# First unit of an attention-plus-experts kernel as eight block products, and the second batch's first two chunks moved to the end of the pair

## Chip, cores and metric

The kernel runs on one core of a Trainium2 chip. The metric is device time in microseconds. Before the change the median of three runs is 1271.27 us (1271.16 to 1274.32).

## What is computed

There are two stages, over 8 batches, 8 heads, 576 tokens and head size 64. Attention runs twice: 32 pack queries p attend to k and v, and the 576 tokens q then attend to the 32 packed rows. The result, laid out as 4608 tokens x 512, goes through four dense experts, weighted by normalised probabilities:

```python
p_packed = sm_attn(p, k, v)
out = sm_attn(q, p_packed, p_packed)          # x: (4608, 512)
p = domain_probs / (domain_probs.sum(-1, keepdims=True) + 1e-09)
for e in range(4):
    h = np.maximum(x @ w1[e], 0.0)            # (4608, 1024)
    y += p[:, e:e+1] * (h @ w2[e])            # (4608, 512)
```

## The kernel before

**Folding.** The second attention has only 32 rows per head, so its value product is folded into w1: `g_form` (line 370) multiplies the packed rows (`ppbd`) with a chunk of w1 and yields `ghl`. The first expert layer then multiplies `ghl` with the softmax weights of the tokens (`xh`, `xl`). Every fp32 operand of the large products is split into a rounded high part (a cast, `hi_of`) and the rest as a low part (a subtraction, `lo_of`), and a product takes three matmuls: high x low, high x high, low x high.

**Units.** The 4 x 1024 hidden columns are cut into eight chunks of 512 (`NCH`). A *unit* is one chunk of one batch: `units` (lines 403 and 404) lists (pair of batches, chunk, batch). Before the change the list begins with batch 0's chunks 0 and 1, batch 1's chunks 1 and 0, and goes on chunk by chunk, batch 0 and 1 in turn; the three later pairs run through chunks 0 to 7.

**First layer.** `mm1_group(u, kh, c)` (line 422) makes one of four blocks of a unit's hidden matrix, half `c` of the tokens (288 columns) by half `kh` of the chunk: 12 matmuls, then one VectorE instruction (relu and probability, from `pbt`). The blocks are a11, a12 (left token half) and a21, a22 (right).

**Second layer.** A unit's product with w2 has the same 2 x 2 block form and is done with seven products instead of eight, in the order `ORDER` (line 35): a11, s3, s1, s2, a22, s4, a12, where the s are sums and differences of the blocks. `s_operand` (line 472) splits an operand, cast on ScalarE and subtraction on GpSimd; `split` (line 414) does it for a12, with the subtraction on VectorE. `product(u, i)` (line 535) issues 12 matmuls; the first of a batch is copied into an accumulator (`acc`), later ones are added by VectorE. The last unit alone uses eight block products, summed in PSUM (`last_unit`, line 577). `combine` (line 607) makes the four output blocks from the seven accumulators at a batch's end.

**Weights.** `t_form` (line 504) makes the seven prepared forms of a w2 chunk (`tt`): seven casts on ScalarE, seven subtractions and four differences on GpSimd. In the first pair each chunk's forms are made and stored to `td` in DRAM (`t_store`); the later pairs load them (`t_load`). The pool has ten `tt` buffers, the raw w2 halves (`rw0`, `rw1`) one each, raw w1 (`wraw`) four.

**The opening** (lines 664 to 721) runs batch 0's attention, with the tokens in halves (`tok_halves`, line 303), loads batch 1's, makes chunk 0's forms, folds chunk 0 for batch 0 and issues the four first-layer groups of unit 0. The left token half's groups, a11 and a12, can run before the right half's softmax is done.

**Order.** TensorE's order is that of the text: `together` (line 121) closes what came before it, `mm` adds to it. `InOrder` fixes VectorE's and GpSimd's order in the opening while `on` is set; `Behind` keeps attention and preparation behind the sums. The loop at line 743 runs the units: product i, the operand two products ahead, parts of the fold (`gsteps`), the next unit's groups (`GROUPS`), a step of the second batch's or the next pair's attention (`back`), and a step of `t_form` (`FORM`). SP issues nearly all DMAs, in order.

## Time and profile before

| what | value |
| --- | --- |
| median of three runs | 1271.27 us |
| lowest, highest run | 1271.16, 1274.32 us |
| profiled execution, its own time | 1272.35 us |
| span of the profiled execution | 1270.6 us |
| mean granted TensorE clock | 0.997 |
| TensorE, VectorE, GpSimd, ScalarE busy | 98%, 73%, 58%, 39% |
| DMA read, written | 173.35 MB, 38.87 MB |

All durations in the rows belong to the one profiled execution. The page names a group by line, engine, operation and tiles; the line of a matmul is that of the helper that issued it (L116 the plain ones, L119 transposes, L124 those issued together), L68 is the helper that fixes an order, so groups are best told apart by tiles: `dbl` is any PSUM tile, `st` and `stl` split operands, `ablk` and `sblk` blocks and sums, `ghl` the folded w1, `xh` and `xl` the token weights, `pbt` the probabilities, `rw` raw w2, `wraw` raw w1. PE is TensorE, PEld its weight load, DVE VectorE, ACT ScalarE, POOL GpSimd, SPq SP's queue. Matmuls overlap, so the busy time of one is longer than the distance to the next.

### The profile page before, as it was taken

Reading aid. Unit: us, or ns where it says so; the run is one execution under the profiler, and the core shown is the slowest. Engines: PE = TensorE matmul, PEld = TensorE weight load, DVE = VectorE, ACT = ScalarE, POOL = GpSimd, SP = SyncE. Lnnn points to the kernel's source line nnn. Section 1 sums busy time; section 2 is a strip of 40 time slices with the busy share of each in tenths; the row PEclk is TensorE's granted clock in tenths of the full one; section 3 lists DMA queues with packets and bytes.
Section 4 is the critical chain, followed back from the end, with each engine's and each line's share of the span. In section 5 each row is a group of like instructions: output and inputs, shape, how many; then the busy total and the mean of one; then the engine's idle time right before and its main releaser. Section 6 shows DMA issues by size and latency. Waiting matters only on the chain.

```text
span 1270.6 us, 26902 instructions
## 1 busy us (share of the span) xinstructions
PE 1247.0 (98%) x10732; PEld 1166.7 (92%) x10732; DVE 926.1 (73%) x1389; ACT 496.1 (39%) x847; POOL 735.8 (58%) x529
## 2 busy tenths in 40 slices
PE   6899999999999999999999999999999999999998
PEld 3789899999999999999999999999999999999998
DVE  6675676788876667888777676788877567766766
ACT  2554445344435233343335433243343533323331
POOL 3876978798675344455466344364557545445456
PEclk9899999999999999999999999999999999999999
DMA  9665575536466444555345555433445543444322
GB/s 339 242 250 200 218 236 177 193 123 213 161 211 209 163 160 127 181 175 165 125 150 175 175 196 165 159 115 116 159 159 182 159 139 116 123 151 159 126 67 76
DMA packets 86508, 213.98 MB, mean 168 GB/s; under 512 B 8816, under 2 KB 27632, under 8 KB 86384
## 3 DMA queue, kind: packets, MB, share of 16 engines
q1 hardware_dynamic: 85712, 212.11, 50.3%
q8 instruction: 86, 1.41, 0.5%
q14 instruction: 38, 0.31, 0.1%
q10 hardware_dynamic: 672, 0.15, 0.1%
HBM read 173.35 MB, written 38.87 MB: 167 GB/s over the span
## 4 chain that ended last, share of the span: by engine, by line
PE 91%; POOL 2%; DMA 2%; DVE 2%; issue 1%; ACT 0%; SPq 0%; DVEq 0%; POOLq 0%; ACTq 0%
PE dbl L116 85%; PE dbl L124 6%; POOL st L68 1%; DMA rw<-in_w 1%; PE dbl L119 1%; DMA pbt<-pnd 1%; DMA vt<-in_v 1%; DVE a L68 1%; POOL tt L68 1%; POOL acc L68 0%; DVE dbl L68 0%; DVE sblk L68 0%; DVE s L68 0%; POOL rw L68 0%; ACT st L151 0%
## 5 line engine op out<-in xcount | busy, mean ns | idle before, releaser
L116 PE MATMUL dbl<-st,tt 128*128 128x288 f32 x4608 | 665.7, 295 | 3.5 <-DVE acc L68 1.8
L116 PEld LDWEIGHTS dbl<-st,tt 128*128 128x128 f32 x4608 | 623.1, 188 | 38.6 <-POOL st L68 19.2
L68 POOL TENSOR_TENSOR st<-sblk,st 128x576 fp32r<-128x576 f32 x252 | 364.7, 1458 | 435.9 <-ACT st L151 434.6
L116 PE MATMUL dbl<-xh,ghl 128*128 128x288 f32 x2048 | 414.4, 295 | 0.0
L68 DVE TENSOR_TENSOR acc<-dbl,acc 128x576 f32<-128x576 f32 x390 | 292.3, 750 | 93.0 <-PE dbl L116 90.6
L116 PEld LDWEIGHTS dbl<-xh,ghl 128*128 128x128 f32 x2048 | 328.9, 189 | 0.2 <-DVE ghl L68 0.2
L116 PE MATMUL dbl<-xl,ghl 128*128 128x288 f32 x1024 | 303.3, 296 | 6.0 <-POOL xl L68 5.7
L151 ACT CAST st<-sblk 128x576 fp32r<-128x576 f32 x252 | 164.1, 675 | 362.6 <-DVE sblk L68 290.9
L68 POOL TENSOR_TENSOR st<-ablk,st 128x576 fp32r<-128x576 f32 x128 | 187.2, 1463 | 47.8 <-ACT st L151 47.7
L116 PEld LDWEIGHTS dbl<-xl,ghl 128*128 128x128 f32 x1024 | 193.1, 189 | 8.7 <-POOL xl L68 6.4
L68 DVE SCALAR_TENSOR_TENSOR dbl<-dbl,pbt 128x576 f32<-128x576 f32 x128 | 97.8, 764 | 75.7 <-PE dbl L116 74.5
L68 DVE SCALAR_TENSOR_TENSOR ablk<-dbl,pbt 128x576 f32<-128x576 f32 x128 | 96.4, 753 | 65.5 <-PE dbl L116 63.0
L151 ACT CAST st<-ablk 128x576 fp32r<-128x576 f32 x128 | 86.1, 674 | 123.7 <-PE dbl L116 92.4
L116 PE MATMUL dbl<-stl,tt 128*128 128x288 f32 x780 | 114.6, 296 | 0.0
L116 PEld LDWEIGHTS dbl<-stl,tt 128*128 128x128 f32 x780 | 105.9, 188 | 0.2
L68 DVE TENSOR_TENSOR ghl<-dbl,ghl 128x512 fp32r<-128x512 f32 x128 | 84.9, 685 | 25.9 <-ACT ghl L151 25.9
L151 ACT CAST ghl<-dbl 128x512 fp32r<-128x512 f32 x128 | 72.2, 590 | 52.9 <-DVE ghl L68 52.2
L68 POOL TENSOR_TENSOR tt<-rw,tt 128x512 fp32r<-128x512 f32 x57 | 74.2, 1321 | 18.7 <-ACT tt L85 18.7
L68 DVE TENSOR_TENSOR stl<-dbl,stl 128x576 fp32r<-128x576 f32 x64 | 48.4, 756 | 39.5 <-ACT stl L151 39.5
L124 PE MATMUL dbl<-wraw,ppbd 64*32 64x512 f32 x1024 | 67.7, 595 | 0.9 <-DMA wraw<-in_w 0.9
L462 ACT COPY sblk<-dbl 128x576 f32<-128x576 f32 x63 | 40.4, 642 | 64.1 <-DVE sblk L68 64.1
L552 ACT COPY acc<-dbl 128x576 f32<-128x576 f32 x56 | 35.9, 641 | 50.9 <-PE dbl L116 50.8
(64 smaller groups left out, 703.1 us busy)
## 6 DMA issues: line engine op xcount, KB each, us to landing
tt<-td SPq DMA_DIRECT2D x175, 512.0 KB, 4.3
wraw<-in_w SPq DMA_DIRECT2D x132, 256.0 KB, 4.3
td<-tt SPq DMA_DIRECT2D x56, 512.0 KB, 5.0
pbt<-pnd SPq DMA_DIRECT2D x32, 288.0 KB, 3.9
out<-acc SPq DMA_DIRECT2D x31, 288.0 KB, 2.6
rw<-in_w SPq DMA_DIRECT2D x16, 512.0 KB, 5.8
kt<-in_k SPq DMA_DIRECT2D x14, 576.0 KB, 5.2
kt<-in_q SPq DMA_DIRECT2D x14, 576.0 KB, 5.8
```

The costliest lines, as they stand in the source:

```text
L68: res = getattr(self.eng, op)(*args, **kw)
L116: on_pe(nc.tensor.matmul(**kw))
L119: on_pe(nc.tensor.transpose(**kw))
L124: ins = nc.tensor.matmul(**kw).ins
L151: return eng.copy(out=dst, in_=src)
L462: nc.scalar.copy(out=held("s1"), in_=psv)
L552: nc.scalar.copy(out=accs[b, i], in_=psv)
```

## The change

- Ten matmuls of the identity with itself are issued as soon as the identity is made, into a PSUM tile that nothing reads.
- In the opening w1's chunk 0 is loaded ahead of w2's, and batch 0's probabilities ahead of batch 1's keys and values. Batch 1's pack scores leave the opening.
- Chunk 0 of w2 is prepared as four plain blocks (`raw_form`: four casts on ScalarE, four subtractions on GpSimd) instead of seven forms.
- Unit 0 uses eight block products (`first_unit`), each pair summed in PSUM: four on the left token half right after a11 and a12, four on the right half between unit 1's first-layer groups. Their results go straight into the four accumulators that `combine` turns into output blocks. The subtractions for a11 and a12 are on GpSimd.
- Batch 1's chunks 0 and 1 move behind chunk 7 of the pair. Chunk 0's seven forms are made there, from a second load of w2; folds for batch 1 alone stand in units 12 and 13. The second pair begins with chunk 1, which is still in the buffers.
- Probabilities are keyed by batch and expert, and the loop's special cases for the first four units become those for the first two.

The diff, cut to its core:

```diff
+FIRST = 10
...
+    ps = dbl()
+    for _ in range(FIRST):
+        nc.tensor.matmul(out=ps[:, 0, 0:P], lhsT=ident, rhs=ident, start=True, stop=True)
...
-    units = [(0, 0, 0), (0, 1, 0), (0, 1, 1), (0, 0, 1)]
-    units += [(sb, ch, 2 * sb + i) for sb in range(SB) for ch in range(2 if sb == 0 else 0, NCH) for i in range(2)]
+    units = [(0, 0, 0), (0, 1, 0)]
+    units += [(0, ch, i) for ch in range(2, NCH) for i in range(2)]
+    units += [(0, 0, 1), (0, 1, 1)]
+    units += [
+        (sb, ch, 2 * sb + i) for sb in range(1, SB) for ch in ((1, 0, *range(2, NCH)) if sb == 1 else range(NCH))
+        for i in range(2)
+    ]
...
-        lo_of(st[:, 1], psv, st[:, 0], vec)
+        lo_of(st[:, 1], psv, st[:, 0], gq if u == 0 and name in ("a11", "a12") else vec)
...
+    def raw_form(ch):
+        raw = [w2r.pop((ch, kh)) for kh in range(2)]
+        for name in ("b11", "b12", "b21", "b22"):
...
+            hi_of(t[:, 0], src, nc.scalar)
+            lo_of(t[:, 1], src, t[:, 0], gq)
+            tt[ch, name] = t
+            yield
...
+    def first_unit():
+        sb, ch, b = units[0]
+        pss = {}
+        for left, n in (
+            ("a11", 1), ("a12", 1), ("a11", 2), ("a12", 2), ("a22", 1), ("a21", 1), ("a22", 2), ("a21", 2),
+        ):
+            r, kh = int(left[1]) - 1, int(left[2])
+            opens = left in ("a11", "a22")
+            st, t = blocks[0, "op", ORDER.index(left) if left in ORDER else left], tt[ch, f"b{kh}{n}"]
+            if opens:
+                pss[r, n] = dbl()
...
+            if not opens:
+                acc = new_acc(b, ORDER.index(RESULT[r, n - 1]))
+                if (r, n) == (1, 1):
+                    nc.scalar.activation(out=acc, in_=ps[:, :, 0:HS], func=AF.Copy, scale=-1.0)
+                else:
+                    nc.scalar.copy(out=acc, in_=ps[:, :, 0:HS])
+                if (r, n) == (1, 2):
+                    other = accs[b, ORDER.index(RESULT[0, 1])]
+                    vacc.tensor_tensor(out=other, in0=other, in1=ps[:, :, 0:HS], op=ALU.subtract)
+            yield
...
+        raws = w1_load(0)
         for kh in range(2):
             w2_load(0, kh, raw_tile)
-        forms = t_form(0, True)
-        raws = w1_load(0)
+        forms = raw_form(0)
         drain(wavefront(packs[:2], 1))
+        load_probs(0, 0)
         for i in (2, 3, 2, 3):
             next(packs[i])
-        load_probs(0, 0)
...
         drain(fold)
         next(halves)
-        next(forms)
-        mm1_group(0, 0, 0)
-        s_operand(0, 0)
-        next(halves)
-        mm1_group(0, 1, 0)
-        for gen in packs[2:]:
-            next(gen)
-        mm1_group(0, 1, 1)
-        mm1_group(0, 0, 1)
-        s_operand(0, 1)
-        vq.on = gq.on = False
-        drain(forms)
+        splits = [mm1_group(0, kh, 0, False) for kh in range(2)]
+        for ready in splits:
+            ready()
+        drain(halves)
...
+    direct = first_unit()
+    for _ in range(4):
+        next(direct)
+    mm1_group(0, 1, 1)
+    mm1_group(0, 0, 1)
+    tsteps = t_form(1)
+    next(tsteps)
+    drain(g_form([0], 1, raws))
+    raws = w1_load(2)
...
+    for i in range(4):
+        next(direct, None)
+        for grp in GROUPS_FIRST[i]:
+            mm1_group(1, *grp)
+        if i:
+            s_operand(1, i - 1)
+        for _ in range((0, 2, 2, 3)[i]):
+            next(back)
+        next(tsteps)
...
+        if u == 1:
+            gsteps, gat = g_form([0, 1], 2, raws), (2,)
+        elif u == 13:
             gsteps, gat = g_form([1], 1, raws), (0,)
+        elif not odd and u + 2 < len(units):
+            gsteps = g_form([1] if u == 12 else [units[u + 2][2], units[u + 3][2]], units[u + 2][1], raws)
+        fch = 2 if u == 1 else (ch + 1) % NCH if sb == 0 and u < 14 else None
...
-            if u < 2 or sb == 0 and u > 3 and not odd:
+            if sb == 0 and (u == 1 or not odd):
                 t_store(ch, i)
-            if u == 2:
-                t_load(0, i)
-            elif odd and not opening and fch is None:
+            if nxt[1] != ch and (nxt[1], i) not in tt:
                 t_load(nxt[1], i)
```

## Rows read from the trace of the kernel before

**Rows 1.** The page, part 1: an engine's busy time in us, its share of the span, its instructions.

```profile
PE 1247.0 (98%) x10732; PEld 1166.7 (92%) x10732; DVE 926.1 (73%) x1389; ACT 496.1 (39%) x847; POOL 735.8 (58%) x529
```

**Rows 2.** The page, part 4: the chain that ended last, shares of the span by engine.

```profile
PE 91%; POOL 2%; DMA 2%; DVE 2%; issue 1%; ACT 0%; SPq 0%; DVEq 0%; POOLq 0%; ACTq 0%
```

**Rows 3.** Busy time of each engine in stretches of the span (us, and the number of instructions in brackets), then the granted clock of TensorE as a share of 2.4 GHz, the share of the 16 DMA engines and GB/s. Stretches overlap a transfer's edge, so the DMA share can exceed 1.

```profile
28.55:33.40 4.85, 0.00 (x0) 0.00 (x0) 4.61 (x10) 1.10 (x2) 4.77 (x5) 1.00 1.06 376
33.40:34.19 0.79, 0.00 (x0) 0.00 (x1) 0.76 (x3) 0.16 (x1) 0.74 (x1) 0.50 1.03 384
34.19:40.20 6.01, 5.89 (x21) 5.23 (x22) 4.15 (x11) 3.60 (x8) 4.84 (x5) 0.50 0.92 362
40.20:67.10 26.90, 25.46 (x275) 21.66 (x275) 16.42 (x30) 15.64 (x30) 23.43 (x19) 1.00 0.65 219
67.10:75.00 7.90, 6.11 (x49) 4.46 (x48) 7.90 (x14) 5.72 (x10) 7.90 (x6) 1.00 1.03 409
...
131.00:138.10 7.10, 5.61 (x59) 3.83 (x58) 3.34 (x6) 4.52 (x9) 7.10 (x7) 1.00 0.75 247
...
300.00:1260.00 960.00, 959.77 (x8107) 911.63 (x8106) 711.55 (x1028) 357.24 (x598) 505.74 (x351) 1.00 0.47 151
```

**Rows 4.** The chain that ended last, in order of time, in the steady part: start, us, what.

```profile
1018.75 34.96 PE dbl L116 x264
1053.70 1.88 PE dbl L124 x32
```

**Rows 5.** TensorE's groups by shape between 5 and 9.5 us: operation, count, busy us and mean ns of one, idle time before.

```profile
L124 PE MATMUL dbl<-kt,pt 64*32 64x288 f32 x32 | 4.3, 683 | 5.3 <-DMA kt<-in_k 5.2
L119 PE MATMUL dbl<-ident,a 128*128 128x128 f32 x1 | 0.3, 328 | 0.0
```

**Rows 6.** The same view between 22 and 25 us.

```profile
L124 PE MATMUL dbl<-xh,pt 64*32 64x288 f32 x32 | 2.3, 407 | 1.3 <-DVE a L68 1.3
```

**Rows 7.** The chain that ended last, in order of time, from 0 to 160 us: start, us, what.

```profile
9.07 7.76 DMA rw<-in_w
...
20.70 7.38 DMA pbt<-pnd
...
131.52 3.85 DMA rw<-in_w
```

**Rows 8.** The timeline of VectorE from 26 to 36 us: start, us, engine, line, operation.

```profile
26.87 0.46 DVE L68 TENSOR_TENSOR a<-a,m 128x288 f32<-128x288 f32 x1
28.17 0.76 DVE L68 SCALAR_TENSOR_TENSOR ablk<-dbl,pbt 128x576 f32<-128x576 f32 x1 [0.84 <-DMA pbt<-pnd]
...
30.02 1.34 DVE L68 TENSOR_TENSOR a<-a,s 128x288 f32<-128x288 f32 x1
...
32.93 0.55 DVE L68 TENSOR_TENSOR a<-a,s 128x288 f32<-128x288 f32 x1
33.52 0.48 DVE L68 STREAM_TRANSPOSE at<-a 128x288 f32<-128x288 f32 x1
```

**Rows 9.** The timeline of GpSimd from 25 to 41 us.

```profile
31.00 1.61 POOL L68 TENSOR_TENSOR st<-ablk,st 128x576 fp32r<-128x576 f32 x1
...
34.54 0.80 POOL L68 TENSOR_TENSOR xl<-at,xh 128x288 fp32r<-128x288 f32 x1 [0.41 <-ACT xh L151]
```

**Rows 10.** The timeline of all engines from 0 to 85 us, rows of TensorE and its weight load and one of ScalarE (its line L151 is the cast to the high part).

```profile
5.19 4.36 PE L124 MATMUL dbl<-kt,pt 64*32 64x288 f32 x32 [5.19 <-DMA kt<-in_k]
...
7.40 0.20 PEld L124 LDWEIGHTS dbl<-kt,pt 64*32 64x32 f32 x8 [1.06 <-DMA kt<-in_k]
...
34.03 0.43 ACT L151 CAST xh<-at 128x288 fp32r<-128x288 f32 x1 [1.70 <-DVE at L68]
...
34.19 0.61 PE L116 MATMUL dbl<-xl,ghl 128*128 128x288 f32 x1 [5.67 <-POOL xl L68]
...
40.63 1.74 PE L116 MATMUL dbl<-st,tt 128*128 128x288 f32 x12
...
44.70 1.31 PE L119 MATMUL dbl<-ident,a 128*128 128x128 f32 x10 [0.48 <-ACT sblk L462]
...
64.08 1.74 PE L116 MATMUL dbl<-stl,tt 128*128 128x288 f32 x12
```

**Rows 11.** Groups of instructions by line, engine, operation and tile over the whole span: count, busy us and mean ns of one, idle time before and what ended it.

```profile
L68 POOL TENSOR_TENSOR st<-ablk,st 128x576 fp32r<-128x576 f32 x128 | 187.2, 1463 | 47.8 <-ACT st L151 47.7
...
L151 ACT CAST st<-ablk 128x576 fp32r<-128x576 f32 x128 | 86.1, 674 | 123.7 <-PE dbl L116 92.4 <-DVE ablk L68 24.4 <-DVE s L68 4.5
...
L68 POOL TENSOR_TENSOR tt<-rw,tt 128x512 fp32r<-128x512 f32 x57 | 74.2, 1321 | 18.7 <-ACT tt L85 18.7
```

**Rows 12.** The timeline from 85 to 115 us: a load of w1 on SP's queue and the next fold on TensorE.

```profile
91.26 1.75 SPq L364 DMA_DIRECT2D wraw<-in_w  x4
...
102.08 1.95 PE L124 MATMUL dbl<-wraw,ppbd 64*32 64x512 f32 x32
```

**Rows 13.** DMA issues: tile, queue, count, KB each, median us from issue to landing.

```profile
tt<-td SPq DMA_DIRECT2D x175, 512.0 KB, 4.3
wraw<-in_w SPq DMA_DIRECT2D x132, 256.0 KB, 4.3
td<-tt SPq DMA_DIRECT2D x56, 512.0 KB, 5.0
```

**Rows 14.** The group of the fold's matmuls on TensorE, from the page's part 5.

```profile
L124 PE MATMUL dbl<-wraw,ppbd 64*32 64x512 f32 x1024 | 67.7, 595 | 0.9 <-DMA wraw<-in_w 0.9
```

More of the change, by code (lines that the diff above doesn't have):

```diff
@@ L356, in tok_halves @@
             normed(g, 1)
-        yield
+            yield
     def w1_load(ch):
@@ L450, in mm1_group @@
         vec.scalar_tensor_tensor(
-            out=held(name) if c == kh else psv, in0=psv, scalar=0.0,
-            in1=pbt[b][:, ts].rearrange("p (o t) -> p o t", o=1).broadcast_to([P, 2, HS]),
+            out=held(name) if (c == 0 if u == 0 else c == kh) else psv, in0=psv, scalar=0.0,
+            in1=pbt[b, ch // (F // FC)][:, ts].rearrange("p (o t) -> p o t", o=1).broadcast_to([P, 2, HS]),
             op0=ALU.max, op1=ALU.mult,
         )
-        if u == len(units) - 1:
+        if u == 0:
+            later = lambda: split(u, name, psv if c else blocks[u, name])
+            if split_now:
+                later()
+            else:
+                return later
+        elif u == len(units) - 1:
             if c != kh:
@@ L502, in raw_tile, with t_form @@
         return wpool.tile(shape, F32, name=name)
-    def t_form(ch, first=False):
+    def t_form(ch):
         raw = [w2r.pop((ch, kh)) for kh in range(2)]
@@ L520, in t_form @@
                 t = wpool.tile([P, 2, 2, DH], F32R, name="tt", bufs=10)
-                hi_of(t[:, 0], blk[of[name]], bpool if first and of[name][0] == "t" else bact)
+                hi_of(t[:, 0], blk[of[name]], bact)
                 tt[ch, ORDER.index(name)] = t
@@ L561, in store @@
         )
-    RESULT = {(0, 0): "a12", (0, 1): "s4", (1, 0): "a22", (1, 1): "s1"}
     def b12_load(ch):
```

122 lines of the change are left out of this document (68 added, 54 removed).

## The prediction, made before the changed kernel was built or run

> **What bounds the kernel now.** I read the page's busy shares first: TensorE is busy for 98% of the span, VectorE 73%, GpSimd 58% [rows 1], and the chain that ended last runs 91% on TensorE [rows 2]. So a microsecond counts only where TensorE is kept from work or given more of it. The stretches show where that is [rows 3]. From 300 to 1260 us it is busy for 959.77 of 960 us; nothing is to be won there. The opening is different: no matmul at all from 28.55 to 34.19 us, a clock of 0.50 (1.2 GHz) until 40.20, and holes at 67 to 75 and 131 to 138 us.
>
> The price of the work comes from the steady part: 264 matmuls of 288 columns in 34.96 us, so 0.1324 us each and 17.5 us for a unit of 132; a fold for two batches takes 1.88 us, one for a single batch half of it [rows 4].
>
> How the hole arises is seen in the chain. The probabilities of the first batch are loaded behind the second batch's keys and values and hold the chain for 7.38 us [rows 7]; VectorE's masked eviction of a11 starts at 28.17 only, and behind it stands the softmax of the right token half, to 34.00 [rows 8]. GpSimd gives the right half's low part at 35.34 [rows 9], and TensorE has waited 5.67 us [rows 10]. During the wait the granted clock fell (at 33.40, 4.85 us after the last matmul ended), so the next 24 matmuls, a22 and a21, took 6.4 us (34.19 to 40.63) where 24 x 0.1324 is 3.2. Only then does the first product begin, since the seven-product form needs all four blocks.
>
> **The change, part by part.** The sum is made inside the profiled execution (1272.35 us, span 1270.6) and applied as a difference to the median, 1271.27, which lies 1.08 below.
>
> *A, the ten matmuls on the identity.* The first scores ran at 683 ns a matmul before the records show a granted clock [rows 5]; the same shape took 407 later [rows 6]. The keys of the second head group land just ahead of 7.40, and its 2.1 us (to 9.55) could become 1.2: at best 0.9 us earlier, all the way down the softmax chain. For the worst: ten at 683 ns one after another from 1.5 us end at 8.3, 3.1 us after the first keys. The nearest row, a 128x128 on the identity, has 328 ns at that clock [rows 5]: 1.5 + 3.3 = 4.8, ahead of the keys at 5.2. I take -0.6; bounds -0.9 and +3.1. So the left-half groups end at 27.9 rather than 28.5. The second batch's scores no longer stand ahead of these groups, but the first groups wait for the last left-half low part on GpSimd anyway; I gain nothing there.
>
> *B, four block products in the hole.* They need only a11 and a12. With the probabilities issued ahead of the second batch's keys, a11's eviction waits for VectorE alone, which is through with the right half's shift at 27.33 [rows 8]; 0.6 earlier, it runs from 26.7 to 27.5. Then the ScalarE cast, 0.67, and GpSimd's subtraction, 1.46 (1.61 in this place) [rows 9, 11]: the first product starts near 29.8, a gap of 1.9 us. It no longer hangs on the softmax. In the long gap of before, the clock was still 2.4 GHz until 33.40 [rows 3], so I put no fall into this one. 48 matmuls x 0.1324 = 6.4: to 36.2. What is late next: a12's eviction now stands ahead of the right half's softmax on VectorE, which took 5.8 us from 28.17 to 34.00, 0.76 of it the eviction. After: 28.65 + 5.1 = 33.7, cast 0.43, low part 0.80 [rows 9]: 35.0, so hidden with 1.2 us to spare. The a22 and a21 groups then run at the full clock, 3.2 us, and end at 39.4 instead of 40.6, with 48 product matmuls done.
>
> *C, to the end of the second unit's first-layer groups.* Before, 40.20 to 67.10. Its 26.9 us hold 135 matmuls (17.9), the fold (0.94), 32 scores (2.3 by rows 6), ten transposes (1.31) [rows 10], and 4.5 us for the value products and for waits: s3, s1 and s2 could be formed only after 40.6. The end row is the seventh product at 64.08 plus two groups' worth of time. After, 96 matmuls are left there, 39 fewer (-5.2), and the 32 scores of the second batch come in (+2.3). Twelve matmuls of extra arithmetic (96 instead of 84, 1.6 us) are counted in this. Of the waits I take 2.5 us as gone (bounds 0 and 4.5): the direct products of the right half need a22 and a21 after an eviction (0.76), a cast (0.67) and a VectorE subtraction of about an eviction's length [rows 8, 11], and the group and fold behind them cover most. So 26.9 - 5.2 + 2.3 - 2.5 = 21.5, from 39.4 to 60.9: **6.2 us ahead** of 67.1. The four-block preparation also replaces seven subtractions and four differences on GpSimd by four subtractions, 4 x 1.32 = 5.3 us [rows 11].
>
> *D, the second unit and the next.* The holes of before, 7.90 - 6.11 and 7.10 - 5.61 [rows 3], make 3.3 us. They come from VectorE and GpSimd being full (7.90 of 7.90), and from the chunk's raw weights landing late, 3.85 us of the chain [rows 7]. After, two units instead of four stand between the opening and chunk 2, so the work is denser: in the second unit GpSimd has five operand subtractions (7.3), eleven preparation steps (14.5) and two attention low parts (2.9), 24.7 us, against TensorE's 17.5 + 1.88 + 2.3 = 21.7. Overrun 3.0. The last prepared weights are needed after six products, 9.5 us into the following unit, so I charge 1.0 of it (bounds 0 and 3.0). D = -3.3 + 1.0 = **-2.3**.
>
> *E, the pair's end.* The work of two units is moved, not added. Extra loads are two of raw w2 and four of w1; seven loads of prepared weights fall away. In the unit of chunk 0, seven stores and seven loads of 512 KB and four loads of 256 KB meet [rows 13]: 8.4 MB, 22.3 us at the 376 GB/s of the opening [rows 3], against 17.5 us. Bounds 0 and +4.8; the loads are issued a unit ahead of need, so I take **+0.3**. Chunk 0's second preparation, in the two units before, is like that of every chunk between: nothing, hidden by VectorE's and GpSimd's room there; without that room up to the 3.0 of D.
>
> Sum: -6.2 - 2.3 + 0.3 = -8.2 us: **1263.1 us**.
>
> **The rivals.**
> *R1, the hole is only made smaller and the clock falls again.* GpSimd has two block subtractions ahead of a11's, and their weights are now loaded behind w1; a raw load held the chain for 7.76 us here [rows 7]. If a11's low part is late by 3 us, and the right half with it, the slow clock costs its 3.2 us again or the gap grows by as much: 1263.1 + 3.2 to 6.4, 1266.3 to 1269.5. For it: the opening's transfers share one full pipe (1.03 to 1.06 of 16 engines from 28.55 to 34.19) [rows 3]. Against: the w1 and w2 bytes are the same, and the hole ends with products that need one block.
>
> *R2, GpSimd and VectorE become the bound in the second and third units.* The overrun of 3.0 is paid in full, the old holes stay: D = +3.0 rather than -2.3, 1268.4, hardly a change. For it: VectorE's 128x288 multiply took 1.34 us at 30.02 and 0.55 at 32.93, and GpSimd's subtraction of 31.00 took 1.61 against a mean of 1.463 [rows 8, 9, 11]. The Trainium skill (SBUF — State Buffer, on the shared port pair) says that a VectorE tensor_tensor with both inputs in SBUF and a GpSimd instruction that reads SBUF exclude each other, the later one waiting to the end of the earlier. The trace agrees in kind, 1.34 against 0.55 us. Against: the direct unit frees some 9 us of GpSimd.
>
> *R3, slower: the one-batch fold at unit 13 waits for w1.* Its four raw tiles are requested only when the fold at unit 12 lets go of the buffers, behind seven stores on SP; the fold is fixed in TensorE's order, so everything stands behind it. If the request goes out only as the fold comes up, as bad as one unit is lost: 1263.1 + 17.5 = 1280.6. It decides the sign from 12.0 us of waiting on (8.2 + 3.8). Against: at 91.26 four such tiles were issued and the fold followed at 102.08, [rows 12], and TensorE's folds waited 0.9 us for w1 in the whole run [rows 14].
>
> *R4, the dummy matmuls do nothing or delay the first scores*: -0.6 lost, or +3.1: 1263.7 to 1266.8.
>
> The Trainium skill (TensorE: Matmul & The Clock Gate, part 1) has the engine start throttled and activity release it, and counts the ramp as under 1% of a span; by it A lies between 0 and -0.9, and the sum between 1263.7 and 1262.8. The 683 ns agree with a slow start; the records give no clock ahead of 9.5 us.
>
> **How the numbers follow.** A measurement of this kernel tells some 0.3%, 3.8 us, from no change: faster is below 1267.5, slower above 1275.1. Chances: my forecast with R4's small ends 0.63 (0.60 of it faster), R1 0.16 (0.11 faster), R2 0.12 (0.04 faster, 0.07 same), R3 0.09 (0.08 slower). So faster 0.75, same 0.16, slower 0.09. The low end is the sum with its good bounds: A -0.3, waits -2.0, D -1.0, E -0.3, -3.6 more, 1259.5, and 1 us for work that I priced too high: 1258.5. The high end takes in R1 and R2: 1270.0.
>
> **What would show it.** Right: matmuls on st begin near 30 us; the idle stretch ahead is under 3 us; the clock stays 1.00 from 10 us on; the second unit's last first-layer group ends near 61; TensorE is busy over 95% from 61 to 130; nothing new near 280 to 330 us. Wrong: clock 0.50 after 30 us (R1), holes of several us between 60 and 100 with GpSimd at 100% (R2), or a TensorE wait for w1 near the end of the first pair (R3).

## The result and the profile after

The changed kernel took **1291.09 us** (median of 4 runs, 1288.54 to 1291.24) beside 1271.37 us for the kernel before (4 runs, 1271.16 to 1274.32): ratio of the means 1.0145, 95% interval [1.0125, 1.0164], so 18.4 us slower (the medians differ by 19.7). The forecast, 1263.1 us with a range to 1270.0 and 0.75 on faster, missed in size and in sign. The profiled execution took 1291.24 us, span 1289.5, which is 18.9 above the span of before.

The page's busy shares and the chain's shares (they answer to [rows 1, 2]):

```profile
PE 1255.0 (97%) x10764; PEld 1176.9 (91%) x10764; DVE 924.7 (72%) x1384; ACT 497.1 (39%) x851; POOL 730.9 (57%) x525
PE 90%; DVE 3%; DMA 2%; issue 2%; ACT 1%; POOL 1%; SPq 0%; DVEq 0%; POOLq 0%; ACTq 0%
```

VectorE's and GpSimd's totals hardly moved, yet TensorE stands idle for 1289.5 - 1255.0 = 34.5 us where it was 1270.6 - 1247.0 = 23.6. Nearly the same work is done (TensorE has 12 matmuls more), in an order that makes TensorE wait. Where, the busy times by stretch show (columns as in [rows 3]):

```profile
18.25:25.01 6.76, 0.01 (x2) 0.00 (x1) 3.33 (x10) 4.34 (x9) 3.28 (x3) 0.84 1.02 342
25.01:33.05 8.04, 6.78 (x24) 5.82 (x24) 6.79 (x12) 1.99 (x4) 4.50 (x4) 0.50 1.07 344
...
67.00:70.60 3.60, 1.06 (x10) 0.83 (x8) 2.19 (x5) 3.57 (x9) 3.60 (x3) 1.00 0.42 152
70.60:74.00 3.40, 3.40 (x50) 2.46 (x49) 1.36 (x6) 1.68 (x6) 3.40 (x4) 0.50 0.81 127
...
99.00:108.10 9.10, 3.75 (x44) 1.80 (x28) 7.77 (x14) 6.69 (x12) 6.26 (x5) 1.00 0.40 129
108.10:115.00 6.90, 4.44 (x18) 4.44 (x19) 2.91 (x5) 1.85 (x4) 6.90 (x6) 0.51 0.19 76
131.00:138.10 7.10, 7.10 (x78) 6.29 (x78) 3.55 (x9) 5.23 (x11) 7.10 (x7) 1.00 0.53 190
...
340.00:350.00 10.00, 7.81 (x75) 5.79 (x74) 9.87 (x13) 4.89 (x8) 10.00 (x8) 1.00 0.95 333
360.00:1260.00 900.00, 900.00 (x7643) 854.12 (x7643) 659.78 (x957) 338.25 (x567) 453.73 (x317) 1.00 0.46 149
```

TensorE waits at 18, 67 and 99 us, each time with the clock at 0.50 (1.2 GHz) behind the wait, and at 340. The hole at 131 of [rows 3] is gone, as forecast; from 360 on TensorE never waits.

To say how much each place costs I added up TensorE's own work. Every matmul is priced at what its shape takes at the full clock (0.1317 us for 288 columns on 128 rows, 1.88/32 for one of the fold, 1.13/32 for one of 32 scores, 0.094 for a transpose, 0.83/40 for the small value products, nothing for the identity's), and what has started up to a time is taken from that time. The result is the **time lost** so far, to holes and to the slow clock together, in us; differences between neighbouring columns are good to some half a microsecond:

| | 45 | 65 | 85 | 105 | 145 | 300 | 360 | 1262 |
|---|---|---|---|---|---|---|---|---|
| before | 29.0 | 32.1 | 34.9 | 36.6 | 39.1 | 42.3 | 43.3 | 53.9 |
| after | 29.7 | 33.5 | 41.1 | 44.2 | 51.9 | 54.8 | 60.4 | 71.2 |
| both queues' order mended | 24.2 | 31.1 | 36.6 | 43.9 | 46.2 | 49.8 | 54.6 | 65.4 |
| all five repairs | 23.8 | 27.9 | 31.2 | 39.7 | 40.5 | 44.0 | 45.6 | 56.3 |
| repairs, attention sooner | 24.8 | 29.0 | 36.0 | 38.7 | 39.4 | 43.2 | 44.4 | 55.1 |
| repairs, less VectorE work | 24.1 | 28.2 | 32.1 | 36.3 | 38.5 | 42.3 | 43.7 | 54.3 |

(The last four rows are kernels of the experiments.) The prices of folds and scores are those of two batches worked on together. A fold of one batch alone took 1.85 us where its price is 0.94 (48.14 to 49.99 us after the change), and the difference stands in the table as lost, as do some 10.7 us from 360 to 1262 in every row, where TensorE never waits; the change moves two such folds from 69 and 90 us to 304 and 325. After against before: 17.3 us more lost by 1262, and 1.6 for the twelve extra matmuls, together the span's 18.9. Of the 17.3, 0.7 is lost by 45 us, 5.5 from 45 to 85, 6.6 from 85 to 145, 4.6 from 300 to 360.

**The opening.** TensorE's timeline (answers to [rows 5, 10]):

```profile
1.36 4.57 PE L140 MATMUL dbl<-ident 128*128 128x128 f32 x20 [1.36 <-POOL ident masks.py:199]
5.86 2.14 PE L125 MATMUL dbl<-kt,pt 64*32 64x288 f32 x32
...
25.01 0.61 PE L117 MATMUL dbl<-xl,ghl 128*128 128x288 f32 x1 [6.75 <-DVE s L69]
...
33.49 3.43 PE L117 MATMUL dbl<-st,tt 128*128 128x288 f32 x24 [1.17 <-POOL st L69]
40.26 4.79 PE L117 MATMUL dbl<-stl,tt 128*128 128x288 f32 x24 [3.34 <-POOL stl L69]
```

The identity's ten matmuls (two records each) run ahead of the first keys and the scores take 2.14 us in place of 4.36. But the left-half groups start at 25.01, where the kernel before started them at 24.98, after an idle stretch of 6.75, and take until 32.33 at the slow clock; a11's products start at 33.49, not 29.8; a12's wait 3.34 more. ScalarE's timeline shows what is late:

```profile
18.80 1.14 ACT L155 CAST tt<-rw 128x512 fp32r<-128x512 f32 x2 [6.07 <-DMA rw<-in_w]
...
21.23 0.77 ACT L333 ACTIVATE a<-a 128x288 f32<-128x288 f32 x2
...
37.54 0.62 ACT L86 CAST tt<-rw 128x512 fp32r<-128x512 f32 x1 [5.58 <-DMA rw<-in_w]
38.07 0.67 ACT L155 CAST stl<-ablk 128x576 fp32r<-128x576 f32 x1
38.64 0.76 ACT L155 CAST xh<-at 128x288 fp32r<-128x288 f32 x2
```

Twice a cast of raw w2 waits for its transfer at the head of ScalarE's in-order queue: for 6.07 us ahead of the softmax's exponentials (21.23; before, 17.87), for 5.58 us ahead of a12's cast and of the right half's. The raw weights are late because of how SP waits. Pieces of the chain that ended last, in order of time:

```profile
4.45 10.06 DMA pnd<-ablk
...
14.52 0.38 SPq L516
...
19.50 9.81 DMA xl<-in_v
...
29.38 8.14 DMA rw<-in_w
...
37.54 0.03 ACT tt L86
```

The load of rw (L516) needs nothing of the probabilities' store, and nothing of the second batch's values; yet it is issued when the one, then the other, has landed. In both places the transfer waited for is the one issued eight before it: the program takes eight DMA semaphores in turn, and a load waits until the last transfer on its own one has landed. The kernel before had the first of these waits too, but a w1 load stood in that place (SP's waits of before, then of after: us in total, times, longest):

```profile
SPq L364 <- DMA pnd<-ablk: 3.0, 1, 3.0
```

```profile
SPq L516 <- DMA pnd<-ablk: 3.2, 1, 3.2
```

In the kernel before, rw was issued at 7.37; in the changed order w1 goes first, and rw at 14.52.

**The second and third units.** TensorE's timeline shows two waits at the end of the second unit's groups:

```profile
65.72 0.40 PE L117 MATMUL dbl<-xl,ghl 128*128 128x288 f32 x1 [1.56 <-DVE acc L69]
...
70.11 2.05 PE L120 MATMUL dbl<-ident,a 128*128 128x128 f32 x10 [2.54 <-ACT a L86]
```

The last of these groups waits 1.56 us for VectorE's accumulation and ends at 67.56 (forecast: 60.9); the transposes behind it wait 2.54 us for exponentials. VectorE reads the second batch's scores, written from 57.06 on, only now:

```profile
66.25 1.41 DVE L69 TENSOR_REDUCE nb<-dbl 128x1 f32<-128x576 f32 x2
```

Until then they hold two of the four PSUM buffers (`ps_dbl`). Then comes the largest loss, in front of the fourth unit, the first of the second batch. The low halves of that batch's tokens, on GpSimd, first in the kernel before, then after (count, ns min/median/max, first and last start):

```profile
L68 POOL TENSOR_TENSOR xl<-at,xh x2: 1425/1430/1434, 75.8 to 79.9; 128x576 fp32r<-128x576 f32 x2
```

```profile
L69 POOL TENSOR_TENSOR xl<-at,xh x2: 1392/1412/1432, 109.1 to 114.3; 128x576 fp32r<-128x576 f32 x2
```

They come 33 us later, and the groups that read them are fixed in TensorE's order, so the products behind them stand too (110.56, 5.01 us idle for xl). The stretch from 85 to 105 us in the kernel before:

```profile
85.00:105.00 20.00, 19.99 (x168) 16.54 (x168) 9.22 (x14) 9.83 (x17) 9.70 (x7) 1.00 0.44 142
```

and after:

```profile
85.00:105.00 20.00, 17.20 (x148) 15.28 (x147) 19.74 (x31) 8.80 (x16) 10.95 (x8) 1.00 0.79 290
```

VectorE was half idle there; now it is full, with the softmax that used to run between 58 and 79.

**The pair's end.** VectorE's timeline:

```profile
328.92 1.67 DVE L69 TENSOR_TENSOR acc<-acc,acc 128x576 f32<-128x576 f32 x1
...
333.30 1.83 DVE L69 TENSOR_TENSOR acc<-acc,acc 128x576 f32<-128x576 f32 x1
335.06 1.99 DVE L69 TENSOR_TENSOR a<-a,s 128x576 f32<-128x576 f32 x1
```

The first batch's closing sums, which came from 349 us on, now come with the batch's last unit two units earlier, together with the next pair's softmax and GpSimd's preparation of chunk 0. Until 340 the two engines are 19.68 and 18.78 of 20 us busy, and TensorE then loses 2.2 us in ten.

### The profile page after: what moved, and what is told of

Its sections match the earlier page's. It is cut to its first block, busy times and chain, and to the rows that moved or that the text cites. A ratio compares the mean times of both kernels' runs of the same rounds, so it can differ in the third digit from the quotient of the medians.

```text
span 1289.5 us, 26929 instructions
## 1 busy us (share of the span) xinstructions
PE 1255.0 (97%) x10764; PEld 1176.9 (91%) x10764; DVE 924.7 (72%) x1384; ACT 497.1 (39%) x851; POOL 730.9 (57%) x525
## 4 chain that ended last, share of the span: by engine, by line
PE 90%; DVE 3%; DMA 2%; issue 2%; ACT 1%; POOL 1%; SPq 0%; DVEq 0%; POOLq 0%; ACTq 0%
PE dbl L117 83%; PE dbl L125 6%; DVE acc L69 1%; PE dbl L120 1%; DMA pnd<-ablk 1%; DMA xl<-in_v 1%; DMA rw<-in_w 1%; DVE sblk L69 1%; DVE a L69 1%; DVE dbl L69 0%; ACT st L155 0%; POOL st L69 0%; DVE ablk L69 0%; DVE m L69 0%; DVE ghl L69 0%
## 5 line engine op out<-in xcount | busy, mean ns | idle before, releaser
L117 PEld LDWEIGHTS dbl<-st,tt 128*128 128x128 f32 x4608 | 625.0, 188 | 39.4 <-POOL st L69 23.9
L69 POOL TENSOR_TENSOR st<-sblk,st 128x576 fp32r<-128x576 f32 x248 | 357.9, 1454 | 450.7 <-ACT st L155 442.3
L69 DVE TENSOR_TENSOR acc<-dbl,acc 128x576 f32<-128x576 f32 (+1 forms) x387 | 290.1, 750 | 96.6 <-PE dbl L117 93.5
L155 ACT CAST st<-sblk 128x576 fp32r<-128x576 f32 x248 | 161.5, 675 | 370.9 <-DVE sblk L69 285.8
L117 PEld LDWEIGHTS dbl<-xl,ghl 128*128 128x128 f32 x1024 | 193.3, 189 | 16.0 <-POOL xl L69 13.2
L69 DVE SCALAR_TENSOR_TENSOR ablk<-dbl,pbt 128x576 f32<-128x576 f32 x128 | 96.3, 752 | 60.4 <-PE dbl L117 57.9
L117 PE MATMUL dbl<-stl,tt 128*128 128x288 f32 x792 | 117.6, 298 | 3.3 <-POOL stl L69 3.3
L117 PEld LDWEIGHTS dbl<-stl,tt 128*128 128x128 f32 x792 | 108.8, 190 | 3.8 <-POOL stl L69 3.6
L69 DVE TENSOR_TENSOR ghl<-dbl,ghl 128x512 fp32r<-128x512 f32 x128 | 85.0, 685 | 21.7 <-ACT ghl L155 21.7
L69 POOL TENSOR_TENSOR tt<-rw,tt 128x512 fp32r<-128x512 f32 x61 | 79.5, 1320 | 23.8 <-ACT tt L155 18.2
L155 ACT CAST ghl<-dbl 128x512 fp32r<-128x512 f32 x128 | 72.2, 589 | 53.9 <-DVE ghl L69 50.8
L69 DVE TENSOR_TENSOR stl<-dbl,stl 128x576 fp32r<-128x576 f32 x63 | 47.7, 756 | 41.1 <-ACT stl L155 41.0
L480 ACT COPY sblk<-dbl 128x576 f32<-128x576 f32 x62 | 39.7, 641 | 65.5 <-DVE sblk L69 65.5
L69 POOL TENSOR_TENSOR acc<-acc,acc 128x576 f32<-128x576 f32 x32 | 49.6, 1563 | 5.1 <-DVE acc L69 5.1
```

The lines of the kernel that those rows point to most:

```text
L69: res = getattr(self.eng, op)(*args, **kw)
L117: on_pe(nc.tensor.matmul(**kw))
L155: return eng.copy(out=dst, in_=src)
L480: nc.scalar.copy(out=held("s1"), in_=psv)
```

## The experiments

Each ratio is taken against runs of the kernel before on the same chip (their medians are 1271.21 to 1272.71). All but three experiments start from the changed kernel. The five single repairs and the first pair of them have two runs each, and their intervals, some 0.003 to 0.004 to either side, overlap that of the changed kernel; what each repair takes away is read from its profile, and only all five together are clear of the changed kernel in time.

### The raw w2 asked for ahead of w1

```
-        raws = w1_load(0)
         for kh in range(2):
             w2_load(0, kh, raw_tile)
+        raws = w1_load(0)
```

> The changed kernel with one thing undone: chunk 0's raw w2 is again loaded ahead of w1. Theory (queues in fixed order): in the changed kernel the w2 load went out at 14.5 us only, since the load in that place of SP's queue waits for the store of the probabilities to land, and the casts of raw w2 stand ahead of the softmax exponentials in ScalarE's queue, so these came at 21.2 instead of about 17.5. Here the w2 load goes out near 7.4, the first exponential runs before 18.5, the left-half groups start before 24 at a clock of 1.00 and the time falls by 5 to 8 us against the changed kernel (1283 to 1286). Rival (the opening is bound by the amount of transfer and by full engines): what w2 gains w1 loses, under 1.5 us (1289.5 to 1291).

1290.75 us, ratio 1.0145 [1.0105, 1.0184]: no gain. ScalarE's timeline:

```profile
15.62 1.14 ACT L155 CAST tt<-rw 128x512 fp32r<-128x512 f32 x2 [2.68 <-DMA rw<-in_w]
...
18.01 0.44 ACT L333 ACTIVATE a<-a 128x288 f32<-128x288 f32 x1
...
36.69 0.62 ACT L86 CAST tt<-rw 128x512 fp32r<-128x512 f32 x1 [7.14 <-DMA rw<-in_w]
37.21 0.67 ACT L155 CAST stl<-ablk 128x576 fp32r<-128x576 f32 x1
```

The first wait is as the theory has it: the exponentials come at 18.01 in place of 21.23, the left groups run from 22.57 to 27.84 (25.01 to 32.33 before the edit) and a11's products begin at 31.08. The second wait then eats nearly all of it: a12's cast is at 37.21, 0.86 earlier. A cause can be shown true and be worth nothing by itself.

### The casts of the next chunk behind those of a11 and a12

```
-        hi_of(st[:, 0], psv, nc.scalar)
+        cast = hi_of(st[:, 0], psv, nc.scalar)
+        if u == 0:
+            order["high"] = cast.ins
...
+    bact.on = True
     tsteps = t_form(1)
```

> The changed kernel with ScalarE's casts of chunk 1's prepared weights put behind the casts of unit 0's blocks. Theory (queues in fixed order): the cast that waited 5.6 us for raw w2 (37.54) no longer stands ahead of a12's cast (38.07) and of the right half's high parts, so a12's products run on without the 3.3 us gap, the clock does not fall a second time, and the right-half groups end 4 to 6 us earlier; the time falls by 3 to 5 us (1286 to 1288). Rival (GpSimd and VectorE are the bound from here on): the prepared weights only come later, 0 to 1 us or slower (1290 to 1292).

1287.75 us, 1.0121 [1.0079, 1.0164]: 3 us better. TensorE's timeline:

```profile
33.89 3.43 PE L117 MATMUL dbl<-st,tt 128*128 128x288 f32 x24 [1.64 <-POOL st L69]
37.15 3.32 PE L117 MATMUL dbl<-stl,tt 128*128 128x288 f32 x24
```

a12's products follow a11's without a gap. Lost at 45 us: 25.7, not 29.7.

### Both

> The changed kernel with both ScalarE waits for raw w2 taken out of the opening: w2's load ahead of w1's, and the casts of chunk 1's prepared weights behind those of unit 0's blocks. Theory (two waits of the same kind in series; the second swallowed what the first one's removal gave): the left-half groups end near 28, the four direct products run from about 31 without a gap over 2 us, and the right-half groups end near 40 as was predicted (47.9 in the changed kernel). Some of the 8 us is lost again at the later stops (64 to 70, 99 to 111): 1282 to 1286. Rival (GpSimd and VectorE or the pipe of transfers bound the opening): right-half groups end no earlier than with the second repair alone (about 43.5), 1286 to 1289.

1285.13 us, 1.0102 [1.0072, 1.0131]: 5.5 us better than the changed kernel, and 5.5 less lost at 45 us. So the first repair has its worth once the second is there. The first product begins at 30.74; the right groups end at 41.8, not near 40.

### The second batch's pack scores sooner

```
-        for _ in range((0, 2, 2, 3)[i]):
+        for _ in range((2, 2, 2, 1)[i]):
             next(back)
```

> The changed kernel with the second batch's attention steps in unit 0 given out as 2, 2, 2, 1 instead of 0, 2, 2, 3, so that its scores are read before a21's sums. Theory (PSUM slots): in the changed kernel the two score tiles hold two of four PSUM slots from 57 to 70 us, until the exponentials behind a21's sums on VectorE, and TensorE loses some 5 us between 64 and 70 and runs at 1.2 GHz after; here that hole is under 2 us and the time falls by 3 to 6 us (1285 to 1288). Rival (VectorE is full there): the sums of a21 come as much later as the softmax comes earlier, 0 to 1 us (1290 to 1291).

1289.39 us, 1.0134 [1.0095, 1.0173]. At 75 us 35.5 is lost, not 39.0, but at 115 it is 50.0 against 51.6: 3.5 gained and half of it given back in the hole at 100, where xl starts at 108.3 and 111.2. In time it is 1.4 us, between what theory and rival had.

### The fourth unit's groups later in TensorE's order

```
-            for grp in (GROUPS_SECOND if u == 1 else GROUPS).get(i, ()):
+            for grp in (GROUPS_SECOND if u in (1, 2) else GROUPS).get(i, ()):
```

> The changed kernel with the first-layer groups for unit 3, the first of the second batch, two products later (steps 3 to 6 of unit 2 instead of 1, 3, 4, 6). Theory (a fixed order on TensorE meets the late token softmax): the stop from 99 to 111 us is a wait of the first of these groups for the second batch's low parts (109.1 to 115.7); with 3 to 4 us more of products ahead of it the stop shrinks to 3 or 4 us, the clock stays at 1.00 and the time falls by 6 to 9 us (1282 to 1285). Rival (GpSimd and VectorE are full and everything behind the stop is late too): the stop only moves to the later products and groups, 0 to 3 us (1288 to 1291).

1287.96 us, 1.0123 [1.0080, 1.0165]: some 3 us, the rival's upper edge and well under the theory's 6 to 9. xl starts at 108.7 and 114.0, as before the edit; TensorE has products of its own to do in the meantime and loses 46.6 by 115 us, not 51.6.

### The first batch's sums two units later

```
-        if final[b] == u and b < B - 1 or u == len(units) - 3:
+        if u == 14:
+            sums, late = combine(0), False
+        elif u != 12 and final[b] == u and b < B - 1 or u == len(units) - 3:
             sums, late = combine(b), b % 2 == 1 and b < B - 1
```

> The changed kernel with batch 0's output sums (seven additions over the accumulators) two units later, in unit 15 instead of unit 13. Theory: the 5 us that TensorE loses between 300 and 360 us, 1 before the change, come from these sums falling together with the making of chunk 0's prepared weights on GpSimd and the next pair's softmax on VectorE; VectorE's additions of two SBUF operands took 1.67 to 1.83 us there. With the sums behind that, TensorE loses under 2.5 us there and the time falls by 3 to 4 us (1287 to 1288). Rival (the loss is that of the seven stores and loads in unit 14, or of the second preparation itself): under 1 us (1290 to 1291).

1287.07 us, 1.0117 [1.0088, 1.0146]: 3.6 us. The two stretches at the pair's end:

```profile
320.00:340.00 20.00, 20.00 (x154) 18.39 (x154) 18.75 (x27) 9.84 (x17) 18.95 (x14) 1.00 0.29 96
340.00:350.00 10.00, 10.00 (x94) 8.45 (x93) 8.61 (x14) 6.64 (x12) 7.32 (x6) 1.00 1.01 376
```

TensorE is full from 340 to 350 with the DMA share at 1.01: the loss there came of the first batch's sums, not of the transfers. From 300 to 360 us 2.7 is lost, not 5.6; two one-batch folds make 1.8 of what is left.

### All five

> The changed kernel with all five repairs: w2 first, casts behind, scores early, groups of unit 3 late, sums later. Theory (the waits are in series, so each repair alone mostly moved the loss to the next): together they give more than the sum of the single gains (0.3, 3.3, 1.7, 3.1 and the sums'): 16 to 22 us against the changed kernel, 1269 to 1275. Rival (VectorE and GpSimd are full in the second and third units, whatever the order): 10 to 13 us, 1278 to 1281, with the holes between 60 and 115 us still there.

1276.75 us (6 runs), 1.0041 [1.0027, 1.0054]: 1.04% below the changed kernel's ratio, 13.2 us, which is what the parts sum to (5.5 + 1.4 + 2.8 + 3.6 = 13.3; each part alone is known less well than that). This is at the rival's 10 to 13, not the theory's 16 to 22, and a hole between 60 and 115 us is still there. TensorE's opening:

```profile
30.89 3.42 PE L117 MATMUL dbl<-st,tt 128*128 128x288 f32 x24 [3.25 <-POOL st L69]
34.15 3.32 PE L117 MATMUL dbl<-stl,tt 128*128 128x288 f32 x24
37.31 0.30 PE L117 MATMUL dbl<-xl,ghl 128*128 128x288 f32 x1
```

This is the opening that was forecast, 1.1 us late: products at 30.89 (29.8), then without a gap the right half's groups at 37.31, at the full clock, ended by 40.6 (39.4). At 45 us 5.2 us less is lost than before. It is gone again by 105, where 8.5 us are lost from 85 on (before: 1.7). That stretch:

```profile
85.00:105.00 20.00, 14.02 (x107) 11.62 (x106) 17.08 (x28) 8.36 (x15) 15.42 (x11) 0.91 0.56 211
```

Neither VectorE (17.08 of 20) nor GpSimd (15.42) is full in it.

### The ten identity matmuls alone, on the kernel before

```
+    ps = dbl()
+    for _ in range(10):
+        nc.tensor.matmul(out=ps[:, 0, 0:P], lhsT=ident, rhs=ident, start=True, stop=True)
```

> The kernel before with only the ten matmuls on the identity added. Theory: the clock is at 2.4 GHz when the second group's scores run, these end at 8.6 instead of 9.6, and the token scores start 0.3 to 0.9 us earlier, but the right half still waits for the probabilities, which are loaded behind the second batch's keys and values, so the time changes by 0 to -0.6 us (1270.6 to 1271.3). Rival: the whole opening moves up by 0.9 us or more (1270.3 or less). If the dummy matmuls delay the first scores: +0.5 us or more.

1272.88 us (8 runs), 1.0003 [0.9991, 1.0014]: nothing that can be measured. In its profile the first reduction of the pack softmax is at 7.66 us, 0.3 later than before.

### What holds the hole that is left: the steps handed out sooner

```
-                for _ in range((3, 1, 1, 2, 2, 1, 1)[i]):
+                for _ in range((4, 2, 2, 2, 1, 0, 0)[i]):
                     next(back, None)
```

(on all five repairs, as are the next two)

> All five repairs (the run before: 1276.75 us) and one more: in the second unit the steps of the second batch's attention are handed out 4, 2, 2, 2, 1, 0, 0 over its seven products in place of 3, 1, 1, 2, 2, 1, 1. If the hole left at 85 to 105 us is a matter of where VectorE's and GpSimd's queues hold the token softmax, the halves xl come some 4 us earlier than 102.45, the hole shrinks from 8.5 us to some 4 and the time is about 1273. Rival: the two engines are full from 76 to 104 and the work only changes places; then what is put forward delays the quotients of the third chunk's weights by as much, and the time stays 1275 to 1279.

1276.26 us (10 runs), 1.0024 [1.0015, 1.0033]: 1.7 thousandths better, 2.2 us. xl:

```profile
L69 POOL TENSOR_TENSOR xl<-at,xh x2: 1427/1432/1437, 92.2 to 95.5; 128x576 fp32r<-128x576 f32 x2
```

They come 10 us earlier, and the hole at 85 to 105 shrinks from 8.5 to 2.7; but 65 to 85 now loses 7.0 in place of 3.3. The order decides where the hole is; the time stays within the rival's 1275 to 1279.

### Without the four differences on GpSimd

```
-                    bpool.tensor_tensor(out=blk[place], in0=blk[x], in1=blk[y], op=ALU.subtract)
+                    if ch != 2:
+                        bpool.tensor_tensor(out=blk[place], in0=blk[x], in1=blk[y], op=ALU.subtract)
```

> All five repairs (1276.75 us), with the four differences of the third chunk's w2 blocks left out of GpSimd's work in the second unit (so the third chunk's products read four tiles that lack these differences). If the hole at 85 to 105 us comes of GpSimd and VectorE being full, some 5 us less work on GpSimd, and as much less stretching of VectorE's subtractions beside it, bring xl forward from 102.45 to about 97, the clock does not fall at 97.7, and the time is about 1269 to 1272. If the hole comes of the order of the queues alone (the softmax steps stand behind the third chunk's work whatever that work takes), xl moves by under 2 us and the time stays 1275 to 1278.

1274.63 us (10 runs), 1.0009 [1.0000, 1.0019]: 3 thousandths better, between the theory's 1269 to 1272 and the rival's 1275 to 1278. The loss from 85 to 105 falls from 8.5 to 4.8, yet xl starts at 100.0 and 105.3, only 2.5 and 0.2 earlier. GpSimd's timeline, and what was waited for between 60 and 108 us:

```profile
90.80 1.87 POOL L69 TENSOR_TENSOR st<-sblk,st 128x576 fp32r<-128x576 f32 x1 [6.37 <-ACT st L155]
```

```profile
POOL st L69 <- ACT st L155: 9.9, 4, 6.4
ACT st L155 <- DVE sblk L69: 6.0, 2, 4.3
```

GpSimd stands for 6.37 us behind a cast of ScalarE that waits for a sum of VectorE. The operand chain of the products (VectorE's sum, ScalarE's cast, GpSimd's low part) is held at its head: VectorE has the softmax in between.

### Less work on VectorE, and the control

```
+            if bs != [1]:
                 m2 = small.tile([P, S // 32, 1], F32, name="m2")
                 avec.tensor_reduce(out=m2, in_=a2, axis=AX.X, op=ALU.max)
                 eng.tensor_tensor(out=a2, in0=a2, in1=m2..., op=ALU.subtract)
```

> All five repairs (1276.75 us), with the shift by the row maximum left out of the second batch's token softmax (two reductions of 0.74 us and two subtractions of 1.1 to 1.7 us, some 4.7 us of VectorE between 76 and 104 us). If the hole at 85 to 105 us is VectorE's queue being full, with the second batch's softmax between the sums that ScalarE's casts and GpSimd's quotients wait for, xl comes some 5 us earlier than 102.45, the loss from 85 to 105 falls from 8.5 us to 4 or less and the time to about 1272. If GpSimd is the bound, VectorE's lighter queue only waits longer, and the time stays 1275.5 to 1278.

1274.10 us (10 runs), 1.0010 [0.9998, 1.0022], 3.1 thousandths below the five repairs; xl starts at 93.9 and 103.3, 8.6 and 2.2 earlier.

The same edit with the steps handed out sooner:

> The same with the second unit's steps handed out 4, 2, 2, 2, 1, 0, 0 (1276.26 us without the cut). There the loss lies at 65 to 85 us (7.0 us) in place of 85 to 105 (2.7 us). If VectorE is the bound wherever the softmax stands, the cut of 4.7 us takes 3 to 4 us of it away: 1272 to 1273. If not, 1275 to 1277.

1274.56 us (10 runs), 1.0016 [1.0006, 1.0026], 0.8 thousandths below the run with the sooner steps: a third of what was expected.

And on the kernel before:

> The control: the kernel before with the same shift left out of the second batch's softmax. VectorE is not the bound there between 60 and 100 us (loss 65 to 85: 2.8 us, 85 to 105: 1.7 us), so the time stays within 0.15% of 1271.9. If VectorE's load is worth time in that kernel too, it falls by 2 us or more, and what the two runs above gain is no sign of the change.

1270.74 us (10 runs), 0.9988 [0.9979, 0.9998]: 1.2 thousandths, 1.5 us, within what the control was to show. Net of it the cut gave the repaired kernel 1.9 thousandths, 2.4 us, which is about as much as the intervals of the three leave open, with the loss at 85 to 105 falling from 8.5 to 4.2; with the sooner steps it gave nothing net. Less work on VectorE and less on GpSimd (4.8, the run without the four differences) thus shrink the hole alike, and some 1.7 us of the 8.5 are a fall of the clock at 97.7 that neither of these two profiles has. Which engine bounds the stretch is not shown; the chain through both is long enough to leave a hole while neither is full. What the 7.0 us at 65 to 85 of the other order hang on was not separated further.

### The hole of before filled, to keep the clock

```
+        for _ in range(18 if (u, kh, c) == (0, 1, 1) else 0):
+            mm(out=ps[:, 0, 0:P], lhsT=ident, rhs=ident, start=True, stop=True)
```

(on the kernel before, ahead of the a22 group's own matmuls)

> The kernel before, with 18 matmuls of the identity on itself ahead of the a22 group of the first unit, into that group's own PSUM tile, in the hole of 5.7 us that the forecast was made from. They take about 4.1 us at the full clock (ten of them took 4.57 us at half) and end near 32.6, ahead of the group's start at 34.19. If what the hole costs is itself plus the fall of the clock behind it, the fall at 33.4 goes, the 24 matmuls behind run at full clock, and the time falls by about 3.2 us, to 1268.1. Rival: the clock falls all the same (or the matmuls end late), and the time stays within 0.1% of 1271.3.

1272.27 us (11 runs), 0.9995 [0.9986, 1.0004]: no change. TensorE's timeline:

```profile
29.89 4.29 PE L116 MATMUL dbl<-ident 128*128 128x128 f32 x36 [0.81 <-DVE ablk L68]
34.73 0.40 PE L116 MATMUL dbl<-xl,ghl 128*128 128x288 f32 x1 [0.56 <-POOL xl L68]
...
35.92 0.40 PE L116 MATMUL dbl<-xl,ghl 128*128 128x288 f32 x1 [0.54 <-POOL xl L68]
...
38.43 0.40 PE L116 MATMUL dbl<-xl,ghl 128*128 128x288 f32 x1 [1.04 <-ACT a L85]
...
40.12 1.75 PE L116 MATMUL dbl<-st,tt 128*128 128x288 f32 x12
```

The clock stays at 1.00 through the hole, and the 24 matmuls do run at full speed. But they now wait for their inputs (0.54, 1.04 us), and the first product begins at 40.12 in place of 40.63 (1.2 us sooner if counted from the left half's groups, which began at 25.65 in this run, 24.98 before). Most of the 3.2 us that the forecast put on the slow clock here were slack: half-speed matmuls were just filling the time until the next operand came.

No version of the change beats the kernel before: the repaired ones that do all the work end at 1.0024 to 1.0041, those that leave some of it out at 1.0009 to 1.0016, and filling the hole of before gives 0.9995.

## Why the prediction was wrong

**A was right in place and worth nothing.** The dummies ended at 5.93, between the bounds, and the first reduction of the pack softmax came 0.3 us earlier (7.11 for 7.39; -0.6 was taken). In the run with them alone it came 0.3 later, so no gain is shown there, and the time is 1.0003.

**B failed on the way to a11's eviction, and on the way from a12's eviction to its products.** The prediction had "a11's eviction waits for VectorE alone", through at 26.7, then a cast and a subtraction by their durations. The last part held: from that eviction to the first product it took 2.98 us (30.51 to 33.49), forecast 3.1. But VectorE was through at 30.5 only. The exponentials came at 21.23, 3.4 later than before, because casts of raw w2 stood ahead of them in ScalarE's queue (the kernel before had one there too, which waited 2.42 us), and VectorE's two shifts of the right half took 2.39 us beside two subtractions of raw w2 on GpSimd (1.11 before). The left groups, behind the long wait, ran at the slow clock and ended at 32.3 for 27.9. a12's cast was put at 0.67 us behind an eviction that ended at 33.1; it began at 38.07, behind the next chunk's cast. The right groups ended at 48.2 for 39.4. R1 named the late w2 and even that it stands behind w1, but priced it as 3 us on a11's low part through GpSimd. The prediction counted casts as instructions (their durations) and did not ask what each would wait for and who stands behind it. With the two queue repairs the first product is 0.9 us late and the right groups 2.4; with all five the landmarks are met to within 1.3 us: left groups to 27.64, first product 30.89, products to 37.47 (36.2), right groups to 40.63, the second unit's groups to 59.77 (60.9).

**B's gain was also mis-sized.** It counted 3.2 us of slow clock as recoverable. Filling the hole shows 0.5 to 1.2 us at the first product, and nothing in the whole. The Trainium skill (TensorE: Matmul & The Clock Gate, HAM oscillation) takes half of the throttled time as the penalty, here by estimate 3.4 us of the 6.8 from 33.40 to 40.20. The measurement says that this is an upper end where operands are late as well.

**C ended late because B did; its own length held.** From the right groups' end to the end of the second unit's groups it took 19.4 us (48.2 to 67.6, the second batch's ten transposes left behind it) and 19.1 with all repairs (transposes in it), where 21.5 was taken, although the one-batch fold, priced at half of 1.88, took 1.85. What C did not have is a wait: it counted the second batch's scores as 2.3 us of matmuls only, and they hold two of the four PSUM buffers until VectorE comes to their reduction. The 1.56 us at 65.72 and, behind C's end, the 2.54 at 70.11 come of it. Handing the steps out sooner takes 3.5 us away.

**D is the term that decided the sign.** -2.3 was taken; between 65 and 145 us the change lost 11.4 us more than before (18.4 against 7.0), some 3.5 of it by those scores. The old hole at 131 to 138 did go. The sum compared GpSimd's work with TensorE's in one unit, 24.7 against 21.7, and charged a third of the overrun. It left VectorE out of that comparison, which is the full one in the changed kernel (19.74 of 20 us), and it left out the order: with two units between the opening and the second batch's first unit, the softmax has to be finished amid the third chunk's preparation, not before it. R2 had the place and the engines right, and too low a price: +3.0 where 11.4 was lost, and 5.6 with all repairs (12.6 against 7.0 from 65 to 145). It added overruns, and left out the chain VectorE, ScalarE, GpSimd in which each waits for the other, which leaves a hole in the repaired kernel though neither VectorE nor GpSimd is full there, and the clock's fall behind a hole.

**E**: +0.3 taken, +4.6 measured from 300 to 360 us, and not by the transfers that it weighed (of its extra loads only the two of raw w2 came; w1's number stayed at 132). Some 1.8 of the 4.6 are the two one-batch folds, which the kernel before paid for at 69 and 90 us. It said that chunk 0's preparation is hidden by VectorE's and GpSimd's room, and did not look at what else the change moves there: the first batch's sums. They start when the batch's last unit ends, which is now two units earlier.

**R3** did not come: no wait for w1 shows at the fold of unit 13. **R4**'s "do nothing" fits the run with the ten matmuls alone; its delay of 3.1 us did not come.

On the stretching of VectorE that R2 cited: in the changed kernel two subtractions a<-a,m took 3.72 us together from 90.49 on, and one a<-a,s that began at 99.89 with GpSimd idle took 0.69. By the Trainium skill (SBUF — State Buffer, on the shared port pair) the later of two such instructions waits to the end of the earlier. The trace agrees, and closely: the first began during a GpSimd subtraction that ended at 91.83 and itself ended at 92.44, the second during one that ended at 93.60 and itself ended at 94.21, each 0.61 us behind. By the 0.69 this is some 2.3 us of VectorE's time in that stretch (an estimate); no run here shows how much of the hole it makes.

The five local causes are shown by edits that took each away in the profile, and their gains in time add up to that of all five, though each alone is within the noise of two runs. What is shown less firmly is the rest. Of the 4.0 us of span between the repaired kernel and before, 1.6 are the extra matmuls and 2.4 lost time; the hole in front of the fourth unit shrinks by about half with less work on VectorE or on GpSimd, and moves with the order; its cause stays open between them. Single profiles also differ in where the clock falls: with the same opening it fell at 26.0 to 29.4 us in one run and nowhere before 97 in another, so a single stretch's loss is good to some 1.7 us.

## What to carry to other kernels

When a change moves work to another engine's in-order queue, write down for each moved instruction what it waits for and what stands behind it: a cast of 0.6 us that waits for a transfer held up its queue for some 6 us, twice. A dense opening has one budget per engine; a gain of 5 us at 45 us was lost by 105, where VectorE and GpSimd had the same work left and less time for it. Before a slow clock or a hole is counted as a gain, look at when the operands after it arrive.

## What the runs showed of the hardware that was not expected

- SP issued a load only after the transfer eight issues earlier had landed, whichever queue had issued it (both used the same one of the program's eight DMA semaphores; that the queue itself has such a limit is not shown): rw at 14.52 behind a store of ScalarE's queue that took 10.06 us for 72 KB, and again at 29.38 behind a load of 9.81 us.
- At the full clock 24 of the 288-column products took 3.43 us, and 6.09 us where the clock had just fallen (the run with w2 first, clock 0.50 from 30.2 to 37.0).
- A gap of 3.25 us in front of the products left the clock at 1.00 in the run with all repairs; one of 2.04 in the run with the sooner steps was followed by 4.97 us for the same 24 matmuls.
- The fold of one batch alone took as long as that of two together: 1.85 us for 16 matmuls (48.14 to 49.99 after the change), 1.88 for 32 [rows 4].
- A VectorE subtraction of two SBUF tiles that began during a GpSimd subtraction ended 0.61 us after that one's end (128x576, at 92.44 and 94.21 after the change), and 0.32 us in the smaller form (128x288, at 29.14 and 30.59).
